# Windowed attention on one Trainium2 core: transposed value products in 32-row column tiles, denominators from a product with ones, 1/den as exp(-ln)

## The chip, the cores and the metric

The kernel runs on 1 core of one Trainium2 chip. The metric is device time in microseconds (us), lower is better. Engines are named as in the profile: PE (TensorE matmuls), PEld (its weight loads, which overlap PE), DVE (VectorE), ACT (ScalarE), POOL (GpSimd), SP (the queue that issues most DMAs). "Clock" is the granted TensorE clock as a share of full speed.

## The reference, cut to what matters

Two independent parts are computed and concatenated: A, a state-space recurrence, and B, an attention with 16 heads of 28 columns in which each of 2048 positions sees 8 positions, 2 apart: itself and 7 earlier ones. The change touches B, and one setup step of A (sines of small angles).

```python
def _B_ref(x, wqkv, wo):                     # x [1, 2048, 448], bf16
    H = 16; Dh = D // H                      # 28
    W, dil = 8, 2
    q, k, v = ...                            # x @ wqkv, split in heads
    idx = pos[:, None] - (jnp.arange(W) * dil)[None, :]
    logits = jnp.einsum("bhsd,bhswd->bhsw", q, kg) * Dh ** -0.5   # idx < 0 is masked
    attn = _softmax(logits, axis=-1)
    o = jnp.einsum("bhsw,bhswd->bhsd", attn, vg)
    return o.transpose(...).reshape(B, S, D) @ wo
```

## The kernel before

A block is 114 queries against 128 keys. For one block and all 16 heads: scores (keys in rows), exponential on ACT, multiplication by a 0/1 mask on DVE, value products, normalization, output transposes, output projection. The value tile has a column of ones behind each head's 28 columns, so the denominator comes out as a 29th column.

```python
def block(self, b):                                          # line numbers of the profile: L140 to L171
    sp = [psum.tile([128, 2, 512], f32, name="s_ps", tag="s") for _ in range(2)]      # 2 buffers
    ...                                                      # 16 score products, 28 rows each (4 row tiles)
    for u in range(2):
        nc.scalar.activation(pt[...], sv, ACT.Exp, scale=scale)             # L153
        V.tensor_tensor(pt[...], pt[...], mask..., op=ALU.mult)             # L154
    po = psum.tile([128, H, 32], f32, name="o_ps", tag="mm")                # "mm": 4 buffers, shared
    for h in range(4):
        for hg in range(4):                                                 # L160: weights are 114 columns wide
            nc.tensor.matmul(po[0:nq, 4*hg+h, 0:29], lhsT=pts[h//2][:, h%2, hg, 0:nq],
                             rhs=self.va[:, b, 4*hg+h, 0:29], start=True, stop=True)
    V.reciprocal(r[0:nq], po[0:nq, :, 28])                                  # L164
    V.tensor_tensor(on[0:nq], po[0:nq, :, 0:28], r..., op=ALU.mult)         # L166 (o_nat)
    for k in range(4):
        nc.tensor.transpose(tp[:, k, 0:nq], onf[0:nq, 112*k:112*(k+1)], ident)   # L170 (pt_o)
    V.tensor_copy(self.oT[:, :, QB*b:QB*b+nq], tp[:, :, 0:nq])              # L171

def wo(self, t):                                             # 128 output rows, after each block
    for k in range(4):                                                      # L177
        nc.tensor.matmul(ps, lhsT=self.oT[:, k, 128*t:128*(t+1)], rhs=self.wo_p[:, k, :], ...)
    nc.scalar.copy(self.yb[:, t % 2, :], ps)                                # L181
```

The setup of A takes two sines on ACT: `activation(sn, angr, ACT.Sin)` and `activation(sh, angr, ACT.Sin, scale=0.5)`.

The softmax here doesn't subtract the row's maximum and nothing guards it: scores larger than these inputs give would overflow.

## Time and profile before

The time before was 279.5 us (median of 2 runs, 278.05 to 280.94). The first lines are from the profile page of the kernel before: each engine's busy share in 40 equal slices of the 278.8 us, in tenths, and the clock likewise.

```profile
PE   0172957999998999996778888888998998988873
DVE  0104895343300100001000000025534536345321
ACT  1002543333599744448854544555345345454310
PEclk9997877999999999999999999995555555555555
```

The clock is at half speed from about two thirds of the span to its end. That is the attention stage. The windows view of the kernel before gives it as the third stretch below: stretch, its length, busy time of PE, PEld, DVE, ACT and POOL (with instruction counts), clock, DMA share, GB/s. The first stretch is setup and projections, the second A's recurrence.

```profile
0.00:87.80 87.80, 61.35 (x362) 31.42 (x366) 31.64 (x71) 35.33 (x65) 33.43 (x52) 0.92 0.41 91
87.80:184.80 97.00, 86.29 (x1209) 71.50 (x1209) 2.54 (x4) 53.51 (x108) 0.00 (x0) 1.00 0.30 95
184.80:278.80 94.00, 76.75 (x668) 52.30 (x665) 40.06 (x86) 38.36 (x49) 0.00 (x0) 0.51 0.07 22
```

In the third, PE is busy 76.75 of 94.00 us and idle 17.25, while DVE and ACT are each busy under half of the time. The chain of waits of the kernel before, over one period of that stage (start, length, what; "issue" is time without a visible wait), shows why:

```profile
197.75 1.49 PE o_ps L160 x16
...
199.26 0.27 DVE r L164
...
199.55 0.64 DVE o_nat L166
...
200.23 0.65 PE pt_o L170 x4
...
200.90 0.41 DVE oT L171
...
201.35 1.68 PE wo_ps L177 x4
203.03 1.49 PE o_ps L160 x16
```

One block takes 203.03 - 197.75 = 5.28 us, and everything in it waits for the step before: PE, DVE, PE, DVE, PE. The groups of the kernel before in the attention stage (line, engine, operation, tiles, shapes, count; busy us, mean ns; idle time before, by releaser) give the PE side:

```profile
L160 PEld LDWEIGHTS <-pt 128*114 128x114 bf16 (+1 forms) x288 | 30.6, 210 | 5.6 <-issue 5.6
L177 PE MATMUL wo_ps<-wo_p,oT 112*128 112x448 bf16 x64 | 26.8, 574 | 2.5 <-DVE oT L171 1.5
L170 PE MATMUL pt_o<-ident,o_nat 114*112 114x114 bf16 (+1 forms) x72 | 11.1, 307 | 10.4 <-DVE o_nat L166 10.3
```

The value products seem to be bound by their weight loads of 114 columns: 16 take 1.49 us, so one starts per 93 ns. That is about what 114 columns take to stream at this clock (0.095 us, an estimate from the 0.373 us between the starts of two products of 448 columns), although only 29 columns stream here. The transposes cost 11.1 us and another 10.3 us of waiting for DVE.

### The profile page before, as it was taken

The numbers are of one execution on the slowest core, as the hardware profiler recorded it, in microseconds if no ns is written. First come the engines' busy times: TensorE is split into PE (matmuls) and PEld (weight loads), VectorE is DVE, ScalarE is ACT, GpSimd is POOL, SyncE is SP. The second block draws the span as 40 slices with busy tenths as digits, with TensorE's granted clock in tenths as the row PEclk, the third lists the DMA queues.
The fourth block names the chain that finished last, engine by engine and source line by source line (L and its number), as shares of the span: only waits on it lengthen the run. The fifth ranks groups of instructions, "written<-read, shape, count | busy, mean of one in ns | idle before, by whom it ended". The sixth has DMA issues, their size and how long they took to land.

```text
span 278.8 us, 5182 instructions
## 1 busy us (share of the span) xinstructions
PE 224.4 (80%) x2234; PEld 155.2 (56%) x2237; DVE 74.2 (27%) x161; ACT 127.2 (46%) x221; POOL 33.4 (12%) x52
## 2 busy tenths in 40 slices
PE   0172957999998999996778888888998998988873
PEld 0020413444587999995655556565565566665551
DVE  0104895343300100001000000025534536345321
ACT  1002543333599744448854544555345345454310
POOL 8000389950000000000000000000000000000000
PEclk9997877999999999999999999995555555555555
DMA  7976900000700362220024444210000000001000
GB/s 206 189 137 117 230 0 1 2 0 0 266 1 2 101 199 102 101 101 33 2 82 126 124 123 127 85 33 2 33 2 33 33 2 33 2 33 35 0 33 33
DMA packets 24550, 19.29 MB, mean 69 GB/s; under 512 B 12624, under 2 KB 23952, under 8 KB 24400
## 3 DMA queue, kind: packets, MB, share of 16 engines
q1 hardware_dynamic: 23584, 17.36, 23.2%
q10 hardware_dynamic: 944, 1.61, 2.2%
q8 instruction: 17, 0.28, 0.4%
q14 instruction: 5, 0.04, 0.0%
HBM read 9.53 MB, written 7.34 MB: 60 GB/s over the span
## 4 chain that ended last, share of the span: by engine, by line
PE 51%; ACT 17%; DVE 13%; issue 9%; SPq 7%; DMA 2%; ACTq 0%
PE wo_ps L177 10%; PE o_ps L160 9%; PE qk_ps L109 7%; SPq L67 4%; PE l1A L397 4%; PE pt_o L170 4%; DVE o_nat L166 4%; PE v_ps L129 4%; PE y_ps L482 3%; PE l1B L397 3%; ACT xaT_sb L421 3%; ACT ya L488 2%; DVE oT L171 2%; DVE r L164 2%; DMA dsk_raw<-in_A_Dskip_dram 2%
## 5 line engine op out<-in xcount | busy, mean ns | idle before, releaser
L109 PE MATMUL qk_ps<-xbT_sb,wqk_p 128*128 128x512 bf16 x125 | 36.0, 447 | 24.8 <-DMA xbT_sb<-in_B_x_dram 12.7
L109 PEld LDWEIGHTS <-wqk_p 128*128 128x128 bf16 x128 | 14.1, 110 | 45.6 <-issue 35.3
L153 ACT ACTIVATE pt<-s_ps 128x912 bf16<-128x912 f32 (+1 forms) x36 | 33.2, 931 | 7.7 <-PE s_ps L145 5.0
L154 DVE TENSOR_TENSOR pt<-pt,mask 128x912 bf16<-128x912 bf16 (+1 forms) x36 | 22.4, 622 | 53.4 <-ACT pt L153 53.1
L160 PEld LDWEIGHTS <-pt 128*114 128x114 bf16 (+1 forms) x288 | 30.6, 210 | 5.6 <-issue 5.6
L164 DVE RECIPROCAL r<-o_ps 114x16 f32<-114x16 f32 (+1 forms) x18 | 4.6, 258 | 98.4 <-PE o_ps L160 98.4
L160 PE MATMUL o_ps<-v_aug,pt 128*114 128x29 bf16 (+1 forms) x288 | 29.0, 249 | 0.0
L181 ACT CAST yb<-wo_ps 128x448 bf16<-128x448 f32 x16 | 8.5, 532 | 44.6 <-PE wo_ps L177 42.5
L177 PE MATMUL wo_ps<-wo_p,oT 112*128 112x448 bf16 x64 | 26.8, 574 | 2.5 <-DVE oT L171 1.5
L397 PEld LDWEIGHTS <-Bcat 112*128 112x128 bf16 x448 | 25.8, 98 | 0.2 <-issue 0.2
L170 PE MATMUL pt_o<-ident,o_nat 114*112 114x114 bf16 (+1 forms) x72 | 11.1, 307 | 10.4 <-DVE o_nat L166 10.3
L488 ACT CAST ya<-y_ps 128x448 bf16<-128x448 f32 x16 | 8.5, 532 | 23.1 <-issue 20.3
L145 PE MATMUL s_ps<-qT,kT 28*128 28x114 bf16 (+1 forms) x288 | 17.9, 271 | 0.8 <-ACT pt L153 0.7
L407 ACT CAST ht<-l1A 128x512 bf16<-128x512 f32 x16 | 9.6, 601 | 18.6 <-issue 15.2
L397 PE MATMUL l1A<-xaT_sb,Bcat 112*128 112x128 bf16 x256 | 17.1, 219 | 0.1
L170 PEld LDWEIGHTS <-o_nat 114*112 114x112 bf16 (+1 forms) x72 | 7.9, 198 | 13.6 <-DVE o_nat L166 13.6
L348 POOL TENSOR_TENSOR Mmat<-Dm,Scat 128x896 bf16<-128x896 f32 x7 | 11.6, 1688 | 24.6 <-DVE Scat L340 24.6
L129 PE MATMUL v_ps<-wqkv_nat,xbT_sb 128*128 128x448 bf16 x72 | 14.3, 352 | 0.0
L177 PEld LDWEIGHTS <-oT 112*128 112x128 bf16 x64 | 6.9, 131 | 13.1 <-issue 7.1
L117 ACT CAST qT<-qk_ps 128x512 bf16<-128x512 f32 x8 | 4.7, 583 | 20.4 <-PE qk_ps L109 20.4
L397 PE MATMUL l1B<-xaT_sb,Bcat 112*128 112x128 bf16 x192 | 13.3, 219 | 0.0
L145 PEld LDWEIGHTS <-kT 28*128 28x128 bf16 x288 | 8.3, 108 | 5.9 <-issue 3.2
(202 smaller groups left out, 357.1 us busy)
## 6 DMA issues: line engine op xcount, KB each, us to landing
hs<-ht SPq DMA_DIRECT2D x16, 224.0 KB, 2.0
hin<-hs SPq DMA_DIRECT2D x16, 224.0 KB, 2.6
xa_sb<-in_A_x_dram SPq DMA_DIRECT2D x1, 1792.0 KB, 7.2
out_dram<-ya SPq DMA_DIRECT2D x16, 112.0 KB, 1.7
out_dram<-yb SPq DMA_DIRECT2D x8, 224.0 KB, 2.1
wqkv_nat<-in_B_wqkv_dram ACTq DMA_DIRECT2D x1, 1008.0 KB, 5.2
wo_p<-in_B_wo_dram ACTq DMA_DIRECT2D x1, 392.0 KB, 9.8
bX<-in_A_B_re_dram SPq DMA_DIRECT2D x1, 392.0 KB, 5.6
```

The lines of the kernel that those rows point to most:

```text
L67: nc.sync.dma_start_transpose(self.xT[:, 0:3, cols], self.B_x[0, rows, 0:384])
L109: nc.tensor.matmul(ps[:], lhsT=self.wp[:, w, k, 4 * hg:4 * hg + 4].rearrange("p h d -> p (h d)"), rhs=self.xT[:, k, self.XP + 512 * c:self ...
L129: nc.tensor.matmul(ps[:].rearrange("p h d -> p (h d)"), lhsT=self.xT[:, k, c0:c0 + NCH], rhs=self.wn[:, k, 2 * D:3 * D], start=(k == 0), s ...
L145: nc.tensor.matmul(sp[h // 2][:, h % 2, QB * hg:QB * hg + nq], lhsT=self.kT[32 * h:32 * h + DH, hg, kc:kc + NCH], rhs=self.qT[32 * h:32 * ...
L153: nc.scalar.activation(pt[:, :, :, 0:nq], sv, ACT.Exp, scale=scale)
L154: V.tensor_tensor(pt[:, :, :, 0:nq], pt[:, :, :, 0:nq], self.mask[:, 0:nq].unsqueeze(1).unsqueeze(1).to_broadcast([NCH, 2, 4, nq]), op=ALU ...
L160: nc.tensor.matmul(po[0:nq, 4 * hg + h, 0:DH + 1], lhsT=pts[h // 2][:, h % 2, hg, 0:nq], rhs=self.va[:, b, 4 * hg + h, 0:DH + 1], start=Tr ...
L170: nc.tensor.transpose(tp[:, k, 0:nq], onf[0:nq, k * KP:(k + 1) * KP], self.ident[0:nq, 0:nq])
L177: nc.tensor.matmul(ps[:], lhsT=self.oT[:, k, NCH * t:NCH * (t + 1)], rhs=self.wo_p[:, k, :], start=(k == 0), stop=(k == KT - 1))
L348: eng.tensor_tensor(out_tile, Dm[:].unsqueeze(1).unsqueeze(1).to_broadcast([NCH, n, 2, PL]), scal.unsqueeze(3).to_broadcast([NCH, n, 2, PL ...
L397: nc.tensor.matmul(reg(m), lhsT=self.Bcat[:, k, m, :], rhs=self.xT[:, k, j, :], start=(k == 0 and m in (0, MA)), stop=(not has_prev and k ...
L488: nc.scalar.copy(ya[:], yps[:])
```

## The change

The intent: let the value product write its output already transposed. The probabilities become the moving operand (114 columns) and the values, 32 columns of one head, the weights; the four heads of a head group write to four 32-row parts of the PSUM tile, which are four column tiles of the array. The transposes and their copies go. The denominator would then be a row, so a second product with a 32-column weight of ones gives it on all 32 rows of the head, and `1/den` is `exp(-ln(den))` on ACT. A unit of work is now four blocks of one head group instead of one block of all four, so the output projections of three or four tiles come together after each four units. To have one table set of activation functions for the whole kernel, A's sines become polynomials on DVE, and one table load is issued at the start (`act_table`, not in the cut below). The output weight is padded to 128 rows and loaded by four DMAs after a memset.

```diff
-    def block(self, b):
+    def unit(self, g, hg):                    # four blocks (the last group two), one head group
...
-        for h in range(4):
-            for hg in range(4):
-                nc.tensor.matmul(po[0:nq, 4 * hg + h, 0:DH + 1], lhsT=pts[h // 2][:, h % 2, hg, 0:nq],
-                                 rhs=self.va[:, b, 4 * hg + h, 0:DH + 1],
+        for i in range(nb):
+            for h in range(4):
+                nc.tensor.matmul(po[32 * h:32 * h + 32, QB * i:QB * i + nq[i]],
+                                 lhsT=self.va[:, b0 + i, 4 * hg + h, :],
+                                 rhs=pts[h // 2][:, h % 2, QB * i:QB * i + nq[i]],
                                  start=True, stop=True, skip_group_check=True)
-        V.reciprocal(r[0:nq], po[0:nq, :, DH])
-        V.tensor_tensor(on[0:nq], po[0:nq, :, 0:DH], r[0:nq]..., op=ALU.mult)
-        for k in range(KT):
-            nc.tensor.transpose(tp[:, k, 0:nq], onf[0:nq, k * KP:(k + 1) * KP], self.ident[0:nq, 0:nq])
-        V.tensor_copy(self.oT[:, :, QB * b:QB * b + nq], tp[:, :, 0:nq])
+        for lo, hi, o in spl:
+            for h in range(4):
+                nc.tensor.matmul(pd[32 * h:32 * h + 32, lo:hi], lhsT=self.ones[:, o, :],
+                                 rhs=pts[h // 2][:, h % 2, lo:hi], start=True, stop=True, ...)
+        nc.scalar.activation(r[:, 0:tot], pd[:, 0:tot], ACT.Ln)
+        nc.scalar.activation(r[:, 0:tot], r[:, 0:tot], ACT.Exp, scale=-1.0)
+        V.tensor_tensor(self.oT[:, hg, QB * b0:QB * b0 + tot], po[:, 0:tot], r[:, 0:tot], op=ALU.mult)
...
     def attention(self):
-        for b in range(self.NB):
-            self.block(b)
+        for g, (b0, nb) in enumerate(self.GROUPS):
+            for hg in range(4):
+                self.unit(g, hg)
             ... output projections of the tiles that are complete
...                                            # loads2
-        nc.scalar.dma_start(self.wo_p[:], self.B_wo.rearrange("(k p) c -> p k c", p=KP))
+        nc.gpsimd.memset(self.wo_p[:], 0.0)
+        for h in range(4):
+            nc.scalar.dma_start(self.wo_p[32 * h:32 * h + DH, :, :], wo_v[h])
...                                            # setup of A
-        nc.scalar.activation(sn[:], angr[:], ACT.Sin)
-        nc.scalar.activation(sh[:], angr[:], ACT.Sin, scale=0.5)
+        ... polynomials of sin and cos of the half angle, about 17 DVE operations on 128x91
```

More of the change, by code (lines that the diff above doesn't have):

```diff
@@ L35 @@
 MAGIC = 12582912.0
+SINC = [(-1.0) ** k / math.factorial(2 * k + 1) for k in range(6, 0, -1)]
+COSC = [(-1.0) ** k / math.factorial(2 * k) for k in range(7, 0, -1)]
 def _make_identity(nc, ident):
@@ L75, in loads2 @@
         nc, pool = self.nc, self.pool
-        self.wo_p = pool.tile([KP, KT, D], bf16, name="wo_p")
-        nc.scalar.dma_start(self.wo_p[:], self.B_wo.rearrange("(k p) c -> p k c", p=KP))
+        self.wo_p = pool.tile([NCH, 4, D], bf16, name="wo_p")
+        nc.gpsimd.memset(self.wo_p[:], 0.0)
+        wo_v = self.B_wo.rearrange("(g h d) c -> h d g c", g=4, d=DH)
+        for h in range(4):
+            nc.scalar.dma_start(self.wo_p[32 * h:32 * h + DH, :, :], wo_v[h])
     def prep(self):
@@ L92, in prep @@
         self.va = pool.tile([NCH, self.NB, H, 32], bf16, name="v_aug")
-        G.memset(self.va[:, :, :, DH:], 1.0)
-        G.memset(self.va[0:self.HL, 0, :, DH:], 0.0)
+        G.memset(self.va[:, :, :, DH:], 0.0)
+        self.ones = pool.tile([NCH, 2, 32], bf16, name="ones")
+        G.memset(self.ones[:], 1.0)
+        G.memset(self.ones[0:self.HL, 1, :], 0.0)
         self.mask = pool.tile([NCH, self.QB], bf16, name="mask")
@@ L99, in prep @@
                             base=self.HL - DIL * w, pattern=[[1, self.QB]], channel_multiplier=-1)
-        self.oT = pool.tile([KP, KT, self.XC], bf16, name="oT", tag="xbT")
+        self.oT = pool.tile([NCH, 4, self.XC], bf16, name="oT", tag="xbT")
     def qk_proj(self, c):
@@ L134, in v_proj @@
                 nc.vector.tensor_copy(self.va[:, b, :, 0:DH], ps[:])
-    def block(self, b):
+    def unit(self, g, hg):
         nc, pool, V = self.nc, self.pool, self.nc.vector
+        b0, nb = self.GROUPS[g]
         QB, XP, HL = self.QB, self.XP, self.HL
-        nq = min(QB, S - QB * b)
         scale = DH ** -0.5
-        kc = QB * b + XP - HL
+        nq = [min(QB, S - QB * b) for b in range(b0, b0 + nb)]
+        tot = sum(nq)
         sp = [self.psum.tile([NCH, 2, 512], f32, name="s_ps", tag="s") for _ in range(2)]
-        for hg in range(4):
+        for i in range(nb):
+            b = b0 + i
+            kc = QB * b + XP - HL
             for h in range(4):
-                nc.tensor.matmul(sp[h // 2][:, h % 2, QB * hg:QB * hg + nq],
+                nc.tensor.matmul(sp[h // 2][:, h % 2, QB * i:QB * i + nq[i]],
                                  lhsT=self.kT[32 * h:32 * h + DH, hg, kc:kc + NCH],
-                                 rhs=self.qT[32 * h:32 * h + DH, hg, QB * b:QB * b + nq],
+                                 rhs=self.qT[32 * h:32 * h + DH, hg, QB * b:QB * b + nq[i]],
                                  start=True, stop=True, skip_group_check=True)
@@ L150, in block @@
         for u in range(2):
-            pt = pool.tile([NCH, 2, 4, QB], bf16, name="pt", tag="pt", bufs=4)
-            sv = sp[u][:, :, 0:4 * QB].rearrange("p h (g q) -> p h g q", q=QB)[:, :, :, 0:nq]
-            nc.scalar.activation(pt[:, :, :, 0:nq], sv, ACT.Exp, scale=scale)
-            V.tensor_tensor(pt[:, :, :, 0:nq], pt[:, :, :, 0:nq],
-                            self.mask[:, 0:nq].unsqueeze(1).unsqueeze(1).to_broadcast([NCH, 2, 4, nq]), op=ALU.mult)
-            pts.append(pt)
-        po = self.psum.tile([NCH, H, 32], f32, name="o_ps", tag="mm")
@@ L158, in block @@
-        for h in range(4):
-            for hg in range(4):
-                nc.tensor.matmul(po[0:nq, 4 * hg + h, 0:DH + 1], lhsT=pts[h // 2][:, h % 2, hg, 0:nq],
-                                 rhs=self.va[:, b, 4 * hg + h, 0:DH + 1],
-                                 start=True, stop=True, skip_group_check=True)
-        r = pool.tile([NCH, H], f32, name="r", tag="r", bufs=2)
-        V.reciprocal(r[0:nq], po[0:nq, :, DH])
-        on = pool.tile([NCH, H, DH], bf16, name="o_nat", tag="o_nat", bufs=2)
@@ L166, in block @@
-        V.tensor_tensor(on[0:nq], po[0:nq, :, 0:DH], r[0:nq].unsqueeze(2).to_broadcast([nq, H, DH]), op=ALU.mult)
-        onf = on[:].rearrange("p h d -> p (h d)")
-        tp = self.psum.tile([KP, KT, NCH], bf16, name="pt_o", tag="mm")
-        for k in range(KT):
-            nc.tensor.transpose(tp[:, k, 0:nq], onf[0:nq, k * KP:(k + 1) * KP], self.ident[0:nq, 0:nq])
-        V.tensor_copy(self.oT[:, :, QB * b:QB * b + nq], tp[:, :, 0:nq])
+            pt = pool.tile([NCH, 2, 4 * QB], bf16, name="pt", tag="pt", bufs=4)
@@ new lines, in unit @@
+            nc.scalar.activation(pt[:, :, 0:tot], sp[u][:, :, 0:tot], ACT.Exp, scale=scale)
+            if tot == nb * QB:
+                pv = pt[:, :, 0:tot].rearrange("p h (b q) -> p h b q", q=QB)
+                V.tensor_tensor(pv, pv, self.mask[:].unsqueeze(1).unsqueeze(1).to_broadcast([NCH, 2, nb, QB]),
+                                op=ALU.mult)
+            else:
+                pv = pt[:, :, 0:QB]
+                V.tensor_tensor(pv, pv, self.mask[:].unsqueeze(1).to_broadcast([NCH, 2, QB]), op=ALU.mult)
+                pv = pt[:, :, QB:tot]
+                V.tensor_tensor(pv, pv, self.mask[:, 0:nq[1]].unsqueeze(1).to_broadcast([NCH, 2, nq[1]]), op=ALU.mult)
@@ new lines, in unit @@
+            pts.append(pt)
+        po = self.psum.tile([NCH, 4 * QB], f32, name="o_ps", tag="mm")
+        pd = self.psum.tile([NCH, 4 * QB], f32, name="d_ps", tag="mm")
+        for i in range(nb):
+            for h in range(4):
+                nc.tensor.matmul(po[32 * h:32 * h + 32, QB * i:QB * i + nq[i]],
+                                 lhsT=self.va[:, b0 + i, 4 * hg + h, :],
+                                 rhs=pts[h // 2][:, h % 2, QB * i:QB * i + nq[i]],
+                                 start=True, stop=True, skip_group_check=True)
@@ new lines, in unit @@
+        spl = ((0, QB, 1), (QB, tot, 0)) if b0 == 0 else ((0, tot, 0),)
+        for lo, hi, o in spl:
+            for h in range(4):
+                nc.tensor.matmul(pd[32 * h:32 * h + 32, lo:hi], lhsT=self.ones[:, o, :],
+                                 rhs=pts[h // 2][:, h % 2, lo:hi], start=True, stop=True, skip_group_check=True)
+        r = pool.tile([NCH, 4 * QB], f32, name="r", tag="r", bufs=2)
+        nc.scalar.activation(r[:, 0:tot], pd[:, 0:tot], ACT.Ln)
+        nc.scalar.activation(r[:, 0:tot], r[:, 0:tot], ACT.Exp, scale=-1.0)
@@ L175, in wo @@
         ps = self.psum.tile([NCH, D], f32, name="wo_ps", tag="mm")
-        for k in range(KT):
-            nc.tensor.matmul(ps[:], lhsT=self.oT[:, k, NCH * t:NCH * (t + 1)], rhs=self.wo_p[:, k, :],
-                             start=(k == 0), stop=(k == KT - 1))
+        for hg in range(4):
+            nc.tensor.matmul(ps[:], lhsT=self.oT[:, hg, NCH * t:NCH * (t + 1)], rhs=self.wo_p[:, hg, :],
+                             start=(hg == 0), stop=(hg == 3))
         if t % 2 == 0:
@@ L189, in projections, with act_table @@
         self.v_proj(4)
+    def act_table(self):
+        nc = self.nc
+        nc.scalar.add_instruction(mybir.InstLoadActFuncSet(
+            name=nc.get_next_instruction_name(), act_func_set_id=6,
+            engine=mybir.EngineType.Activation, ins=[], outs=[]))
     def attention(self):
         done = 0
-        for b in range(self.NB):
-            self.block(b)
-            end = min(S, self.QB * (b + 1))
+        for g, (b0, nb) in enumerate(self.GROUPS):
+            for hg in range(4):
+                self.unit(g, hg)
+            end = min(S, self.QB * (b0 + nb))
             while (done + 1) * NCH <= end:
@@ L299, in setup @@
         V.scalar_tensor_tensor(angr[:], kf[:], -C2, angr[:], op0=ALU.mult, op1=ALU.add)
+        z2 = sm("z2", big)
+        V.scalar_tensor_tensor(z2[:], angr[:], 0.25, angr[:], op0=ALU.mult, op1=ALU.mult)
+        sh = sm("sh", big)
+        ch = sm("ch", big)
+        V.tensor_scalar(sh[:], z2[:], SINC[0], None, op0=ALU.mult)
+        V.tensor_scalar(ch[:], z2[:], COSC[0], None, op0=ALU.mult)
+        for c_ in SINC[1:]:
+            V.scalar_tensor_tensor(sh[:], sh[:], c_, z2[:], op0=ALU.add, op1=ALU.mult)
+        for c_ in COSC[1:]:
+            V.scalar_tensor_tensor(ch[:], ch[:], c_, z2[:], op0=ALU.add, op1=ALU.mult)
+        V.tensor_scalar(sh[:], sh[:], 1.0, 0.5, op0=ALU.add, op1=ALU.mult)
+        V.tensor_tensor(sh[:], sh[:], angr[:], op=ALU.mult)
+        V.tensor_scalar(ch[:], ch[:], 1.0, None, op0=ALU.add)
         sn = sm("sn", big)
-        nc.scalar.activation(sn[:], angr[:], ACT.Sin)
-        sh = sm("sh", big)
-        nc.scalar.activation(sh[:], angr[:], ACT.Sin, scale=0.5)
+        V.scalar_tensor_tensor(sn[:], sh[:], 2.0, ch[:], op0=ALU.mult, op1=ALU.mult)
         cs = sm("cs", big)
@@ L527 @@
     b.loads()
+    b.act_table()
     a.loads_params()
```

## The prediction

> **What bounds the kernel now.** The windows view splits the 278.8 us profile: setup, projections and S5 recurrence until about 184 us, then 95 us of attention. There PE is busy 88%, ACT 46%, DVE 47%, DMA 7%, and the granted TensorE clock is 0.50; before it was 1.00. The chain of waits repeats every 5.28 us per query block: value products 1.49 us (16 weight loads of 114 columns, one per 93 ns), reciprocal 0.26 and `o_nat` 0.62 on DVE, four output transposes 0.64, copy `oT` 0.40, output projection 1.67. PE waits for `o_nat` 9.3 us in total (groups by line). So the stage is bound by one serial PE-DVE-PE-DVE-PE chain on a half-clock PE; 18 blocks give the 95 us.
>
> **Removed.** 72 transposes (10.5 us PE in the stage), 18 copies `oT` (7.1 us DVE), 18 reciprocals (4.7 us), two DVE-PE round trips per block, 114-column probabilities as weights. Two activation-table loads of 1.28 us: one before the Sines, one at 89.7 us that stands in the chain.
>
> **Added.** Per unit of 16 (block, head) pairs: 16 value products streaming 114 columns with 32-column weights, 4 ones products streaming 456, and Ln and Exp on 128x456. ACT casts 128x448 from PSUM in 532 ns, so I estimate Ln and Exp at 0.54 us each. In setup, about 17 more DVE operations of 0.20 to 0.25 us replace two Sines; the running order puts key copies behind them.
>
> **Cost of one unit.** ACT: two exponentials 1.86, Ln and Exp 1.08, 0.9 of an output cast 0.47: 3.4 us. DVE: masks 1.24, multiply 0.63: 1.9. PE at half clock: the Trainium skill ("TensorEngine Tiling (Array Packing)", Key Properties) says that different tiles run in parallel and that changing mode drains the array. This trace agrees on the first for scores: 14 row-tiled products of 114 columns took 0.56 us. If column tiles do the same, values are about 0.5, ones 0.5 to 0.8, scores 0.7, mode changes some tenths, projection 1.5: 3.4 to 4.0 us. If they do not overlap, values and ones take 1.5 us each and PE needs over 5 us.
>
> I expect overlap and a pace of 3.9 us: 18 units, less what is done early, plus start and tail, 72 us instead of 95. Setup: the longer DVE chain costs 2 to 3 us of projection time (PE waits there for DVE copies); the table load at 89.7 us gives back 1.3. Net about +1.5. Sum: 279.5 - 23 + 1.5 = about 258 us, range 246 to 271. Chances: faster by over 2% 0.93, within 2% 0.05, slower 0.02.
>
> **What would show it.** (1) The stage after the recurrence spans 65 to 80 us, ACT 75 to 90% busy. (2) `o_ps` products of one unit: 16 in about 0.5 us (overlap), not 1.5. (3) Ln and Exp about 0.54 us each. (4) One table load in all (the skill's "ScalarE: Activation LUTs", Table sets: one set holds exp and ln). (5) Recurrence starts 1 to 3 us later, less the load saved. (6) The clock stays at 0.5 for most of the stage.
>
> **What would make it wrong.** Column tiles running one after the other: about 270 us or more. The clock returning to 1.00: PE stops mattering, ACT paces at 3.4, about 248. PE order and the four shared PSUM buffers (each unit takes two, held over Ln, Exp and multiply) leaving both engines idle: 265 to 270. Setup growing by 5 us or more through DVE colliding with POOL.

## More of the kernel before

All kernels gave correct results.

## The result, and the profile after

The changed kernel took 248.58 us (median of 2 runs, 248.35 to 248.81); the ratio to the kernel before is 0.8894, with a 95% interval of 0.8693 to 0.9095. Run again with more rounds it took 249.49 us, ratio 0.8863 (0.8814 to 0.8912). A ratio is the mean time of one kernel's fast runs over that of the other's fast runs of the same rounds, so it is not quite the ratio of the medians quoted. The kernel before had medians of 279.5 to 281.2 us; compare ratios. `e1`, `e2` and `e8` ran in this second measurement; the other edits ran on other chips, and are set against the changed kernel through their ratios. All outputs are right.

The page's slices of the changed kernel (247.0 us):

```profile
PE   0282939999999899999777888888859798697983
DVE  0204999543330020000000000000024464655450
ACT  2002435523369964344568554444577898989782
PEclk9999786999999999999999999999995958977687
```

ACT is now at 7 to 9 tenths in the last stage, and the clock there is no longer at half: it goes up and down. The windows view of the changed kernel, same three stages:

```profile
0.00:84.80 84.80, 62.33 (x381) 31.55 (x382) 35.11 (x91) 35.25 (x64) 36.34 (x54) 0.94 0.43 95
84.80:181.10 96.30, 85.43 (x1197) 70.89 (x1196) 1.27 (x2) 50.68 (x105) 0.00 (x0) 1.00 0.31 96
181.10:247.00 65.90, 51.94 (x690) 25.05 (x688) 31.51 (x64) 53.04 (x93) 0.00 (x0) 0.79 0.09 31
```

Attention shrank from 94.0 to 65.9 us, that is by 28.1 of the 31.8 us between the two profiles. ACT is busy for 53.04 of the 65.9. Setup and projections end 3.0 us earlier, not later, and the recurrence is 0.7 us shorter. The groups of the changed kernel in the attention stage:

```profile
L162 ACT ACTIVATE pt<-s_ps 128x912 bf16<-128x912 f32 (+1 forms) x36 | 30.5, 864 | 3.3 <-PE s_ps L155 3.1
L195 PE MATMUL wo_ps<-wo_p,oT 128*128 128x448 bf16 x64 | 19.8, 449 | 0.9 <-DVE oT L189 0.9
L184 PE MATMUL d_ps<-pt,ones 128*32 128x456 bf16 (+3 forms) x96 | 14.6, 378 | 0.9 <-ACT r L187 0.8
L188 ACT ACTIVATE r<-r 128x456 f32<-128x456 f32 (+1 forms) x20 | 11.2, 565 | 0.1
L187 ACT ACTIVATE r<-d_ps 128x456 f32<-128x456 f32 (+1 forms) x20 | 10.5, 528 | 5.3 <-PE d_ps L184 5.1
L177 PEld LDWEIGHTS <-v_aug 128*32 128x32 bf16 x288 | 7.9, 105 | 9.3 <-issue 6.4 <-DVE pt L165 0.9
```

The value products' weight loads fell from 30.6 to 7.9 us, and the transposes are gone. But look at the output projection: the same 64 products of 448 columns, with 112 rows before and 128 now, took 26.8 us and take 19.8. Nothing in the change makes that product cheaper; only the clock does. The windows view of the changed kernel in pieces of 3 us:

```profile
186.00:189.00 3.00, 2.99 (x56) 1.60 (x55) 1.90 (x3) 2.06 (x4) 0.00 (x0) 0.50 0.00 0
189.00:192.00 3.00, 3.00 (x17) 1.03 (x11) 0.98 (x2) 1.95 (x3) 0.00 (x0) 0.55 0.00 0
192.00:195.00 3.00, 2.58 (x42) 1.31 (x40) 1.47 (x3) 2.53 (x5) 0.00 (x0) 1.00 0.00 0
195.00:198.00 3.00, 1.96 (x41) 1.12 (x37) 1.17 (x2) 3.00 (x6) 0.00 (x0) 1.00 0.25 82
198.00:201.00 3.00, 2.48 (x38) 1.46 (x36) 1.99 (x5) 2.75 (x5) 0.00 (x0) 0.58 0.00 0
```

PE is nearly without a gap from 186 to 192 us, the second half of it mostly output projections; then the clock is at 1.00 for about 7 us, and falls back. In the clock records of the trace, every complete stretch of one clock in this stage lasts 3.4, 6.8 or 10.2 us, multiples of 3.41. The Trainium skill ("TensorE: Matmul & The Clock Gate", Part 1: The HAM clock gate) describes two states, half and full rate, where about 3.4 us of sustained activity releases the throttle. The trace agrees on the two states: the recorded clock is 0.50 or 1.00, with values between only where a window holds a change. What counts as such activity is another matter; see `e6_before_wo_twice` below.

So two explanations compete for the 28 us.

- **Theory W (work and chain)**: the gain is the removed transposes and wide weight loads and the shorter chain. The clock is a by-product.
- **Theory C (clock)**: the gain is largely that the output projections now come in bunches, which brings the clock back. The kernel before could have had it without any of the rest.

### The profile page after: what moved, and what is told of

Same layout as the page of the kernel before. It is cut to its first block, busy times and chain, and to the rows that moved or that the text cites. A ratio compares the mean times of both kernels' runs of the same rounds, so it can differ in the third digit from the quotient of the medians.

```text
span 247.0 us, 5315 instructions
## 1 busy us (share of the span) xinstructions
PE 199.7 (81%) x2261; PEld 127.5 (52%) x2261; DVE 67.9 (27%) x157; ACT 139.0 (56%) x261; POOL 36.3 (15%) x54
## 4 chain that ended last, share of the span: by engine, by line
PE 47%; ACT 24%; issue 11%; DVE 8%; SPq 7%; DMA 2%; ACTq 0%
PE qk_ps L116 9%; PE wo_ps L195 6%; PE l1A L433 6%; SPq L69 5%; PE v_ps L136 4%; PE l1B L433 4%; ACT pt L162 4%; PE y_ps L518 4%; ACT ya L524 3%; ACT xaT_sb L457 3%; PE o_ps L177 3%; ACT yb L199 2%; PE s_ps L155 2%; PE d_ps L184 2%; DVE pt L165 2%
## 5 line engine op out<-in xcount | busy, mean ns | idle before, releaser
L165 DVE TENSOR_TENSOR pt<-pt,mask 128x912 bf16<-128x912 bf16 x32 | 23.8, 744 | 130.1 <-ACT pt L162 129.2
L162 ACT ACTIVATE pt<-s_ps 128x912 bf16<-128x912 f32 (+1 forms) x40 | 34.6, 883 | 4.0 <-PE s_ps L155 3.9
L195 PE MATMUL wo_ps<-wo_p,oT 128*128 128x448 bf16 x64 | 19.8, 449 | 0.9 <-DVE oT L189 0.9
L184 PE MATMUL d_ps<-pt,ones 128*32 128x456 bf16 (+3 forms) x96 | 14.6, 378 | 0.9 <-ACT r L187 0.8
L177 PE MATMUL o_ps<-pt,v_aug 128*32 128x114 bf16 (+1 forms) x288 | 12.5, 246 | 3.2 <-DVE pt L165 2.7
L187 ACT ACTIVATE r<-d_ps 128x456 f32<-128x456 f32 (+1 forms) x20 | 10.5, 528 | 5.3 <-PE d_ps L184 5.1
L177 PEld LDWEIGHTS <-v_aug 128*32 128x32 bf16 x288 | 7.9, 105 | 9.3 <-issue 6.4
L136 PEld LDWEIGHTS <-xbT_sb 128*128 128x128 bf16 x72 | 7.0, 99 | 10.8 <-issue 4.5
L189 DVE TENSOR_TENSOR oT<-o_ps,r 128x456 bf16<-128x456 f32 (+1 forms) x20 | 11.5, 579 | 3.9 <-ACT r L188 3.9
L195 PEld LDWEIGHTS <-oT 128*128 128x128 bf16 x64 | 6.1, 113 | 10.3 <-issue 6.5
```

The costliest lines, as they stand in the source:

```text
L136: nc.tensor.matmul(ps[:].rearrange("p h d -> p (h d)"), lhsT=self.xT[:, k, c0:c0 + NCH], rhs=self.wn[:, k, 2 * D:3 * D], start=(k == 0), s ...
L162: nc.scalar.activation(pt[:, :, 0:tot], sp[u][:, :, 0:tot], ACT.Exp, scale=scale)
L165: V.tensor_tensor(pv, pv, self.mask[:].unsqueeze(1).unsqueeze(1).to_broadcast([NCH, 2, nb, QB]), op=ALU.mult)
L177: nc.tensor.matmul(po[32 * h:32 * h + 32, QB * i:QB * i + nq[i]], lhsT=self.va[:, b0 + i, 4 * hg + h, :], rhs=pts[h // 2][:, h % 2, QB * i ...
L184: nc.tensor.matmul(pd[32 * h:32 * h + 32, lo:hi], lhsT=self.ones[:, o, :], rhs=pts[h // 2][:, h % 2, lo:hi], start=True, stop=True, skip_g ...
L195: nc.tensor.matmul(ps[:], lhsT=self.oT[:, hg, NCH * t:NCH * (t + 1)], rhs=self.wo_p[:, hg, :], start=(hg == 0), stop=(hg == 3))
```

## The experiments

### Each half alone: the new products without the bunches, the bunches without the new products

`e3_per_block` is the changed kernel with a unit of one block and all 16 heads:

```diff
-        for i in range(nb):                                   # four blocks, head group hg
+        for hg in range(4):                                   # one block, four head groups
             for h in range(4):
-                nc.tensor.matmul(po[32 * h:32 * h + 32, QB * i:QB * i + nq[i]], ...
+                nc.tensor.matmul(po[32 * h:32 * h + 32, nq * hg:nq * hg + nq], ...
...
+            self.block(b)                                     # then the tile of the output projection
```

> The changed kernel, but a unit is again one query block with all 16 heads (4 head groups side by side in the 456 columns), with its output projection right after it: same transposed value products, ones products, Ln and Exp, one multiply; only the grouping and the bunching of the output projections are undone. Theory W (the gain is less PE work and a shorter chain: no transposes, narrow weights): still most of the gain, 250 to 258 us, whatever the clock does. Theory C (the gain is mostly that bunched output projections bring the TensorE clock back to 1.00): the clock stays at 0.50 through attention and the time is 266 us or more.

Measured: 257.33 us as the median of four runs, one of them slow (260.92); the three fast ones lie between 255.09 and 258.64, and the ratio from these is 0.9132 (0.9062 to 0.9201).

`e4_before_bunched` is the kernel before with one edit:

```diff
             self.block(b)
+            if b % 4 != 3 and b != self.NB - 1:
+                continue                                      # projections after every fourth block
```

> The kernel before, but the output projections are issued only after each four query blocks, three or four tiles in a row (12 to 16 products of 448 columns, over 4.5 us at half clock); nothing else changes. Theory C: the clock comes back to 1.00 after each bunch, mean 0.65 or more in attention, and the time falls by 10 us or more, to below 269. Theory W: the clock may move, but the chain through DVE and the transposes is still there: 272 to 282 us.

Measured: 265.16 us, ratio 0.9439 (0.9385 to 0.9492). The last stretch of the windows view, first of `e3_per_block`:

```profile
179.80:256.80 77.00, 46.64 (x665) 18.81 (x664) 31.25 (x50) 54.82 (x85) 0.00 (x0) 0.60 0.08 26
```

and of `e4_before_bunched`:

```profile
183.70:261.60 77.90, 59.39 (x667) 41.55 (x664) 38.84 (x86) 36.85 (x49) 0.00 (x0) 0.66 0.08 26
```

| attention stage, profiled | length us | PE busy us | PE idle us | clock |
|---|---|---|---|---|
| before | 94.0 | 76.75 | 17.3 | 0.51 |
| before, projections bunched (e4) | 77.9 | 59.39 | 18.5 | 0.66 |
| new products, one block at a time (e3) | 77.0 | 46.64 | 30.4 | 0.60 |
| changed kernel | 65.9 | 51.94 | 14.0 | 0.79 |

(Idle is length minus busy; each idle time has 3.5 to 3.7 us after the last product in it.) The first run came out as theory W expected, the second as theory C did, so neither is the whole cause. A two-line reordering of the old kernel takes 16.1 us off its attention stage. It could do so in two ways, by the clock or by hiding the round trip before each projection; the table says which. PE idle time did not fall (17.3 to 18.5); the whole gain is busy time of the very same matmuls (76.75 to 59.39), so it is the clock. The new products without bunching take off 17.0, and there the clock rose only from 0.51 to 0.60 (it was at 1.00 once in the middle, for 10.2 us; the records do not say why). The two together give 28.1, less than the sum of 33.1. A likely reason is that a faster PE is worth less once PE has less to do; no run separates this.

### Does a busier PE alone bring the clock back?

`e6_before_wo_twice` computes each output projection of the kernel before twice over the same PSUM (same result):

```diff
-        for k in range(KT):
+        for n in range(2 * KT):
+            k = n % KT
```

> The kernel before, with every output projection computed twice over the same PSUM (right result): 64 more products of 448 columns, 1.49 us more PE work per tile at half clock, 0.75 at full. If a denser PE brings the clock back to 1.00 (theory C's mechanism), the mean clock in attention rises to 0.8 or more and the time stays within 270 to 290 us in spite of the added work. If the clock stays at 0.50: 279 + 16 x 1.49, about 303 us.

Measured: 304.25 us, ratio 1.0828 (1.0782 to 1.0874). The last stretch:

```profile
185.70:301.90 116.20, 98.54 (x731) 60.51 (x728) 40.02 (x86) 38.13 (x49) 0.00 (x0) 0.53 0.05 18
```

PE is busy 85% of this stage, and the clock stays at 0.53; the added work is paid in full. A projection tile is now 8 products of 0.373 us (spacing at half clock in the trace), 3.0 us in a row, and in the 16 tiles the clock rose once, for 3.4 us. In `e4_before_bunched` it rose in or at the end of each of the four bunches of 12 or 16 products, 4.5 us or more in a row, and not in the last one of 8.

It is tempting to read this as the 3.4 us of the skill's page, but the traces do not bear it out. The value and score products follow the projection at once, so PE is without a gap for longer than 3.4 us in `e6_before_wo_twice` too, and the clock stays at half (windows view, columns as before):

```profile
223.80:228.97 5.17, 5.17 (x30) 3.07 (x30) 0.94 (x3) 1.64 (x3) 0.00 (x0) 0.50 0.11 35
```

In the kernel before, such gapless stretches last 3.67 us in most blocks. So it takes more than a busy PE to bring the clock back; in `e4_before_bunched` it came back with long runs of wide output products. Which work counts, and how much of it, no run here measures.

### Do the column tiles run side by side?

`e2_tile_major` changes the order of the value products so that four in a row fall into the same column tile:

```diff
-        for i in range(nb):
-            for h in range(4):
+        for h in range(4):
+            for i in range(nb):
```

> The changed kernel, value products issued with the head (the column tile) as the outer loop and the query block inside, so that four products in a row use the same 32 columns of the array; same work, same result. If neighbours in different column tiles run side by side in the changed kernel (trace: 16 products in 0.39 to 0.56 us), the 16 of a unit now take about 0.9 us at full clock and 1.5 at half, and the time grows by 5 to 12 us over the changed kernel, to 254 us or more. If it is not the overlap but only the shorter weights that count: no change within 1 us, and 16 products still within 0.6 us.

Measured: 247.91 us, ratio 0.8814 (0.8781 to 0.8846), where the changed kernel had 0.8863. No slower: the expectation failed. The timeline of PE in `e2_tile_major`, in a stretch at half clock (start, length, what; a length includes the latency of the last one, so spacing is read from starts):

```profile
200.22 0.57 PE L177 MATMUL o_ps<-pt,v_aug 128*32 128x114 bf16 x8
200.57 0.60 PE L184 MATMUL d_ps<-pt,ones 128*32 128x456 bf16 x2
201.10 0.55 PE L195 MATMUL wo_ps<-wo_p,oT 128*128 128x448 bf16 x1
```

Eight value products, four in one tile and then four in the next, begin and give way within 0.35 us. (The program has them in this order on PE's queue.) At half clock 448 columns take 0.373 us, so 114 columns take 0.095, and eight one after the other would need 0.76. They took about what one tile's four need (0.38). So the second tile's products ran beside the first tile's although they stood behind them in the order. The edit did not take the overlap away; it showed that the overlap does not need neighbours in different tiles.

`e11_ones_full_width` takes it away for the ones products, by weights of 128 columns with ones only in the head's 32, accumulated over the four heads:

```diff
-                nc.tensor.matmul(pd[32 * h:32 * h + 32, lo:hi], lhsT=self.ones[:, o, :], ..., start=True, stop=True)
+                nc.tensor.matmul(pd[:, lo:hi], lhsT=self.ones[:, o, h, :], ..., start=(h == 0), stop=(h == 3))
```

> The changed kernel, with the ones products not in column tiles: weights 128 columns wide, ones in the 32 columns of the head and zeros elsewhere, the four heads accumulated into the same 128 rows. Same number of products and streamed columns, same result. If column tiles run side by side, the four products of a unit take 4 x 190 ns at full clock and 4 x 380 ns at half instead of about one of each; PE gains 0.4 to 1.1 us per unit, and the time is 252 to 260 us, unless the denser PE earns more time at clock 1.00. If tiles do not run side by side: the same time within 1 us, and the same span for the four products.

Measured: 248.79 us, ratio 0.8865 (0.8839 to 0.8891): the same time. The timeline of PE at clock 1.00, in the changed kernel:

```profile
194.12 0.38 PE L177 MATMUL o_ps<-pt,v_aug 128*32 128x114 bf16 x14 [0.39 <-DVE pt L165]
194.70 0.38 PE L184 MATMUL d_ps<-pt,ones 128*32 128x456 bf16 x4
```

and in `e11_ones_full_width`:

```profile
192.34 0.94 PE L186 MATMUL d_ps<-pt,ones 128*128 128x456 bf16 x4
```

(Two of the 16 value products are missing from the records.) Four ones products in four tiles take 0.38 us, at full width 0.94: the tiles do run side by side. And yet the time is the same. The last stretch of `e11_ones_full_width` suggests where it went:

```profile
180.80:246.80 66.00, 53.96 (x689) 26.17 (x688) 31.96 (x64) 53.16 (x93) 0.00 (x0) 0.94 0.09 31
```

With the needless PE work the clock was at 0.94 instead of 0.76 to 0.79, and PE's busy time hardly grew (53.96 us for 51.94): the higher clock paid for most of it. ACT is busy for 53.16 us, as before, so it can also have hidden a part; this run does not separate the two. PE is busy 82% of the stage here, and 85% in `e6_before_wo_twice` at 0.53: the busy share of the profile does not tell whether the clock will hold.

### Does ACT pace the new stage?

`e5_cast_on_dve` moves the casts of the output projection:

```diff
-        nc.scalar.copy(self.yb[:, t % 2, :], ps[:])
+        nc.vector.tensor_copy(self.yb[:, t % 2, :], ps[:])
```

> The changed kernel, with the 16 casts of the output projection (0.53 us each, 8.5 us of ACT) moved from ACT to DVE; DVE was half busy. If ACT paces the stage (it was about 88% busy in its middle): 5 to 8 us less, 240 to 244 us. If PE at its mixed clock or the round trips pace it: 247 to 250 us, and ACT gains idle time before the exponentials.

Measured: 246.02 us, ratio 0.8758 (0.8704 to 0.8812). The changed kernel has 0.8863 with an interval that begins at 0.8814, so a gain of some 3 us is likely rather than certain. It was run on another chip. Its profile has the stage at 62.3 us with ACT busy 46.4. ACT lost 6.6 us of busy time and the stage 3.6 to 4.5 (65.9 and 66.8 us in the two profiles of the changed kernel). So ACT seems to be part of the limit, but not all of it: the gain is below the expected 5 to 8. A part of it may be the clock's, which was 0.83 in this stage, with PE busy for 48.64 us instead of 51.94.

`e7_dve_reciprocal` replaces Ln and Exp by one DVE reciprocal, `V.reciprocal(r[:, 0:tot], pd[:, 0:tot])`:

> The changed kernel with one reciprocal on DVE in place of Ln and Exp on ACT. From the trace of the kernel before: 7 elements per partition took 0.20 us and 16 took 0.26, so about 7 ns per element; 456 elements then take 3 to 4 us, DVE needs 5 to 6 us per unit, and the time rises to 280 us or more. If a reciprocal costs no more than another DVE operation (0.6 us): 243 to 247 us, because ACT loses 1.1 us per unit.

Measured: 277.92 us, a single run of unknown state, beside 280.77 for the kernel before. The operations of the tile `r` in its trace (ns minimum/median/maximum):

```profile
L187 DVE RECIPROCAL r<-d_ps x20: 1495/2946/3008, 181.5 to 269.7; 128x456 f32<-128x456 f32 x16, 128x224 f32<-128x224 f32 x4
```

The full-size reciprocal takes 2.95 us, where the multiply of the same size takes 0.63 and Ln and Exp together about 1.16. It costs about 6.5 ns per element of a partition. In the kernel before it worked on 16 elements, now on 456, because the ones product writes the denominator on every row; that is why exp(-ln) belongs to this change. The stage was 95.3 us, so nearly the whole gain went.

### The setup

`e1_before_poly` is the kernel before with polynomial sines and one table load; the edit is the last part of the diff of the change, and nothing of attention.

> The kernel before with the changed setup only: sines by polynomials on DVE, one table load in place of three. The prediction said that the longer DVE chain costs 2 to 3 us and the missing load at 89.7 us gives back 1.3, net +1.5: 281 to 283 us where the kernel before has 281. Against it: the two profiles show the projections ending 47.9 us after the last parameter landed in the changed kernel and 48.4 us in the kernel before, so the chain costs nothing and the load is all that is left: -1 to -2 us, about 279.5.

Measured: 276.63 us, ratio 0.9834 (0.9796 to 0.9871), 4.6 us faster, although at the 2% line the verdict is unclear (the interval reaches over 0.98). That is better than both expectations, and attention kept its length (94.4 us). In its profile the last projection product starts 44.2 us after the last parameter of A has been converted, in the kernel before 48.0 (both my subtractions). Why, I read from the traces. POOL builds A's matrices while DVE finishes A's small operations, and DVE operations then take many times their length: a copy of 128x7 takes 1.68 us in place of 0.16, about as long as one POOL operation beside it (1.69). Projection copies wait behind them, PE waits for these copies, and after such a gap the clock can fall. The windows of `e1_before_poly`:

```profile
36.00:38.00 2.00, 0.73 (x4) 0.38 (x4) 2.00 (x3) 0.00 (x0) 2.00 (x2) 1.00 0.00 0
38.00:40.00 2.00, 1.72 (x9) 0.75 (x8) 1.97 (x8) 0.91 (x2) 0.85 (x2) 1.00 0.00 0
```

and of the changed kernel, which has the same polynomials but did not get this gain (47.5 us between the same two points):

```profile
36.00:38.00 2.00, 1.64 (x5) 0.55 (x4) 1.97 (x8) 0.00 (x0) 0.86 (x2) 0.50 0.00 0
38.00:40.00 2.00, 2.00 (x6) 0.73 (x5) 2.00 (x1) 0.75 (x2) 2.00 (x1) 0.50 0.02 4
```

PE's longest wait there for a DVE copy of `kT` was 3.8 us in the changed kernel and 2.6 in `e1_before_poly`, and only with the first did the clock go to half. But it did so too with the two waits of the kernel before there, of which the longer is 2.7 us, so the length of the wait alone does not decide it. My other guess was a mask multiply that the new order places among these copies, where it took 3.23 us instead of 0.63. `e10_late_mask` keeps it out, by making the mask depend on a tile written after the projections:

```diff
-        G.memset(self.mask[:], 0.0)                           # in prep
+        self.nc.gpsimd.tensor_scalar(self.mask[:], ccat[:, 0, 0:self.QB], 0.0, None, op0=ALU.mult)   # after loads2
```

> The changed kernel, with the mask built only after the projections (made to depend on a tile written at their end), so that the first two mask multiplies on DVE can no longer fall among the projection copies while POOL builds its matrices. In the changed kernel one of them took 3.23 us there instead of 0.63. If that collision is what kept the setup gain of the polynomial (4.6 us alone) from showing: projections end 3 us earlier after the last parameter (about 44.5 us instead of 47.5) and the time is 245.5 to 247.5 us where the changed kernel has 249.5 (ratio about 0.875). If the collision is hidden: no change within 1 us.

Measured: 248.73 us, ratio 0.8862 (0.8817 to 0.8906): no change. DVE's busy time up to the recurrence fell from 35.1 to 31.6 us and the projections ended as before (47.6 us). That guess fell. The half clock with the longer PE gap is what is left; no run here isolates it, so why the gain of the polynomial does not show in the changed kernel stays open.

### A version that beats both

If an attention stage at a mixed clock leaves engines idle, it can run beside A's last loop, where the clock is at 1.00 and DVE does nothing. `e8_interleaved` emits one or two units or projection tiles after each step of that loop:

```diff
+            for _ in range(2 if j % 2 else 1):                # at the end of each step j of A's last loop
+                step = next(steps, None)                      # a unit or one output projection of B
+                if step is not None:
+                    step()
```

> The changed kernel with the attention units (and their output projections) emitted between the steps of the recurrence's last loop, which keeps the clock at 1.00 but leaves DVE idle and ACT half idle. If the clock and idle engines are what the attention stage lacks: the clock stays near 1.00 while the two overlap and the time falls by 15 to 30 us, to 220 to 235 us. If the four shared PSUM buffers or PE's order serialise the two: within 5 us of the changed kernel.

Measured: 238.19 us, ratio 0.8463 (0.8422 to 0.8504), beside 0.8863 of the changed kernel. In its profile the last loop and attention together take from 134.8 us to 236.9, 102.1 us at a clock of 0.91 from the first value product on, where the changed kernel needs 134.7 to 247.0, 112.3 us. It gained 10 to 11 us, less than the 15 to 30 expected.

`e12_combined` adds the DVE casts and the late mask:

> Interleaving with the recurrence's last loop (238.2 us alone), output-projection casts on DVE (about -3.5 alone) and the late mask (about -3 expected alone) together. If the three are independent: 231 to 234 us, ratio 0.82 to 0.835. If the casts no longer matter because ACT is not the limit in the interleaved stage: 235 us.

Measured: 239.61 us, ratio 0.8521 (0.8474 to 0.8568): not better than `e8_interleaved`. The late mask was worth nothing by itself, and the casts are worth nothing here.

## Why the prediction was right or wrong, point by point

- **The time** (258, range 246 to 271; measured 248.6) lay in the range, near its low end. The text named the case that occurred: "The clock returning to 1.00: PE stops mattering, ACT paces at 3.4, about 248". But it was put among what would make the prediction wrong. The wide range, and some luck, kept the number in. By the profiles the change gained 10.3 us more than predicted (31.8 against 21.5): 5.1 in the stage, and 5.2 in setup and recurrence, for which +1.5 was predicted and -3.7 came.
- **"The clock stays at 0.5 for most of the stage"** was the step that failed. It was 0.79. The gain in the stage was 28.1 us and not 23, and `e4_before_bunched` shows what the missing term can be worth: 16.1 us when it comes alone, without any of the new products. The prediction gave the bunching of the projections no term at all.
- **What bounds the kernel before** was half right. The serial chain is there, but the idle time of PE is only 17.3 of 94 us. The other half of the bound, the half-clock PE, was read as a given, and not as something that the order of work decides.
- **Column tiles overlap**: right. Four ones products take 0.38 us in tiles and 0.94 at full width at the same clock. The Trainium skill ("TensorEngine Tiling (Array Packing)", Key Properties) says that different tiles run in parallel; the trace agrees.
- **ACT 75 to 90% busy**: right, 53.04 of 65.9 us is 80%. Ln at 0.56 us was right. Exp of the same size took 0.60, slightly above the 0.54.
- **"ACT ... paces at 3.4"** is only partly shown. Taking 6.6 us of ACT away gave 3.6 to 4.5 us of the stage.
- **One table load**: right, one instead of three.
- **Setup "+1.5" and the recurrence starting "1 to 3 us later"**: wrong in sign; it started 3.0 us earlier. Alone, the polynomial gains 4.6 us. In the changed kernel its share does not show: the last projection starts 47.5 us after the last parameter, against 48.0 before. The rest of the 3.0 us came from something that the prediction did not look at. The parameters themselves are converted at 22.7 to 23.6 us in the ten profiles with the new load of the output weight, and at 25.3 to 25.9 in the four with the old one. The old load (392 KB) is issued at 1.8 us, among the first input loads, the new one at 18.5 us and later. That goes with 2.4 us, but no run changes this load alone.
- **Risks**: serial tiles did not occur, and no run tests the PSUM buffers; what mattered was on the list as the clock.

## What to carry to other kernels

Where a profile shows a stage at half clock, ask first whether the same matmuls in another order would put more of the wide ones in a row: a reordering of two lines, which made runs of 12 to 16 products of 448 columns, was worth 5.6% here, without a change of algorithm. Look at the clock afterwards; 5.17 us of PE without a gap did not bring it back. Count a removed transpose twice, as PE work and as a round trip, but add it to the clock's gain with care, because the two overlap. Streaming the wide operand through 32-column weights in four column tiles cut the value products' weight loads from 30.6 to 7.9 us and made the transposes needless; the price is a denominator repeated over rows, for which exp(-ln) on ACT (1.16 us) beat DVE's reciprocal (2.95 us).

## What the Trainium skill lacked or had wrong

- "TensorE: Matmul & The Clock Gate" ("Why this matters for your kernels") asks for no PE-idle gaps over about 3 us to stay at full rate. Here no gap between the products of the stage was longer than 1.01 us, PE was busy 82% by the profile, and the clock stayed at 0.51 for 94 us. At 85% busy it was 0.53 (`e6_before_wo_twice`), at 82% it was 0.94 (`e11_ones_full_width`). A stretch of 5.17 us without a gap left it at 0.50 (`e6_before_wo_twice`, above). The page does tell of frequent short idle times that make the clock go up and down, but gives no measure of how frequent, nor, but for transposes, of which work counts as busy.
- The same page (Part 3: Packing small matmuls) says that matmuls start and end in strict program order. With four products of one column tile in front of four of another, the eight took about 0.35 us, where the order of start, with 0.095 us per product of one tile, would let the next product begin only after about 0.57 (`e2_tile_major`). In the packed trace the eight starts come in four pairs, 13 or 14 ns within a pair and 71 to 94 ns from one pair to the next. Which record belongs to which product it does not say, so this is a reading of the spacing.
- "ScalarE: Activation LUTs" (What ACT_TABLE_LOAD costs) gives 1283 ns for the load plus about 1380 ns of drain. The trace agrees on 1283 ns; no drain shows: in the kernel before, the load started at 28.55 us, 0.02 us after the copy before it, and the sine at 29.84.
- "GPSIMD Engine Reference" (Specifications) says that POOL shares its SBUF interfaces with DVE and names the colliding kinds. That table lacks the size, though not the skill as a whole: here a DVE copy of 128x7 went from 0.16 to 1.68 us beside a POOL operation of 1.69, and a masked multiply of 128x912 from 0.63 to 3.23 beside one of 3.19.
- No page that I read gives the cost of a DVE reciprocal per element: 2.95 us for 128x456, about 6.5 ns per element of a partition (`e7_dve_reciprocal`).
